# Spectral sequence product: upper rows taken from the lower rows' two sums and one product with the difference of mirrored rows

## Chip, core and metric

The kernel runs on one core of one Trainium2 chip. TensorE (PE) multiplies, ScalarE (ACT), VectorE (DVE) and GpSimd (POOL) work on elements, SyncE (SP) issues all DMAs of the main path from one queue. The metric is the device time of one execution in microseconds (us); the profile's span is the time from the first to the last instruction of one profiled execution.

## Reference

Two independent layers read their own inputs; their outputs stand side by side in a 2048 x 896 result.

```python
S, D, H = 2048, 448, 16
# A: real part of a two-dimensional Fourier transform, by given matrices
a = A_x @ A_dft_hid_re.T
b = A_x @ A_dft_hid_im.T
yA = A_dft_seq_re @ a - A_dft_seq_im @ b
# B: full attention with 16 heads of 28
q, k, v = heads(B_x @ B_wqkv)
yB = concat(softmax(q @ k.T * 28 ** -0.5) @ v) @ B_wo
out = concatenate([yA, yB], axis=-1)
```

The matrices are inputs: `A_dft_seq_re[t, s] = cos(-2 pi t s / 2048)`, `A_dft_seq_im` the sine, in fp32.

## The kernel before

All fp32 data that goes through PE's fast format (`fp32r`) is split into a rounded part `hi` and a rest `lo = x - hi`; a product of two such operands is made of three: hi x hi, hi x lo, lo x hi. The exact fp32 format is used for the sums of attention alone.

Nothing orders the work at run time. While the program is built, a small planner (`Schedule`, L180) keeps a list of tasks for each engine, with a key, a cost and buffers, and emits the instructions in the order in which its own clock lets them run. Each engine then works through its list in that order and waits on semaphores. The costs (`M512`, `M448`, `ACT_S`, ...) and due times (`T_ATT`, `T_END`, `T_FILL`, `T_OUT`, L436) steer only that order.

- **Attention.** For each head, 16 tiles of keys x 4 chunks of 512 queries: a score product (L865), its exponential on ACT (L869), and the sums with v, exact fp32, four 32-row column groups side by side (`quad`, L842, products at L848). The sums are gathered in runs of `run_size` tiles, 8 at first and 10 from 230 us of the plan (`RUN_AT`, L40). `first_tiles` finds each query's offset with transposes and maxima on DVE. `out_of` (L889) takes a head's sums, stores their reciprocals to HBM (L897, L899), reads them spread (L903), multiplies on POOL (L910) and stores the head (L912).
- **Fill.** Everything else on PE fills the gaps between score products: the projections (L581), the values, layer A's transform along the hidden dimension (`hidden`, L682: 16 row tiles of 11 products), and along the sequence (`sequence`, L704). It uses PSUM banks of its own (`fill_s`, `NFILL` = 2).
- **The sequence product.** Part 0 multiplies `wre` by `a`, part 1 `wim` by `-b`. Each part has 16 output tiles of 128 rows; each tile has four steps `q`; each step loads one piece of the matrix (128 x 4 x 128, 256 KB) into `wraw`, splits it (`Piece`, L517: `hi` on ACT L524, `lo` on POOL L530) and issues 12 products of 448 columns (L718). Part 0 stores its tile to HBM (`y_d`, L733); part 1 loads it (L735), adds (L736) and stores the output (L738).
- **Output of attention.** After the last head, for four chunks of 512 rows: load (L967, L972), split (ACT L985, then POOL or DVE), 11 products for each of 16 tiles (L1003), eviction, store (L1011).
- **Check.** A flag (`flag`, L1015) from the sums' and values' ranges decides at the end whether the general path `any_scores` runs instead.

## Time and profile before

| | |
|---|---|
| median of 3 runs | 1010.52 us (1010.41 to 1010.74) |
| the profiled execution | 1010.87 us, its span 1009.2 us |
| granted TensorE clock | 1.000 |
| HBM traffic | 89.92 MB read, 33.69 MB written |
| score exponentials (L869) | 944 in 510.2 us busy |
| sequence products (L718) | 1024 with `whi`, 512 with `wlo` |

The page's busy shares are of the span. A matmul group's mean is the length of one in the pipeline; how far apart they are issued is read from the chain that ended last, printed in order of time.

### The profile page before, as it was taken

Reading aid. Unit: us, or ns where it says so; the run is one execution under the profiler, and the core shown is the slowest. Engines: PE = TensorE matmul, PEld = TensorE weight load, DVE = VectorE, ACT = ScalarE, POOL = GpSimd, SP = SyncE. Lnnn points to the kernel's source line nnn. Section 1 sums busy time; section 2 is a strip of 40 time slices with the busy share of each in tenths; the row PEclk is TensorE's granted clock in tenths of the full one; section 3 lists DMA queues with packets and bytes.
Section 4 is the critical chain, followed back from the end, with each engine's and each line's share of the span. In section 5 each row is a group of like instructions: output and inputs, shape, how many; then the busy total and the mean of one; then the engine's idle time right before and its main releaser. Section 6 shows DMA issues by size and latency. Waiting matters only on the chain.

```text
span 1009.2 us, 16013 instructions
## 1 busy us (share of the span) xinstructions
PE 1002.2 (99%) x5638; PEld 735.8 (73%) x5638; DVE 318.2 (32%) x607; ACT 711.8 (71%) x1410; POOL 364.8 (36%) x339
## 2 busy tenths in 40 slices
PE   9999999999999999999999999999999999999997
PEld 7896667777766876687668666766786677667897
DVE  6362425251505042402314151614041242300111
ACT  7128778798767876796669778877786687667242
POOL 6110234353324333442325443524333253443530
PEclk9999999999999999999999999999999999999999
DMA  8764455324233333333233424242443343243463
GB/s 297 267 202 126 155 180 166 97 77 114 71 100 98 119 89 107 96 114 95 87 104 117 132 67 121 88 118 81 140 104 107 104 141 105 75 125 122 137 198 108
DMA packets 109909, 124.84 MB, mean 124 GB/s; under 512 B 48640, under 2 KB 61440, under 8 KB 109824
## 3 DMA queue, kind: packets, MB, share of 16 engines
q1 hardware_dynamic: 109824, 123.78, 40.7%
q8 instruction: 45, 0.74, 0.3%
q14 instruction: 40, 0.33, 0.1%
HBM read 89.92 MB, written 33.69 MB: 122 GB/s over the span
## 4 chain that ended last, share of the span: by engine, by line
PE 97%; DMA 1%; SPq 0%; DVE 0%; issue 0%; ACT 0%
PE bank L718 31%; PE bank L865 23%; PE bank L848 22%; PE bank L581 16%; PE bank L1003 4%; PE bank L806 1%; DMA kept<-wqkv 1%; DMA kept<-xb 1%; SPq L488 0%; DVE big L427 0%; SPq L559 0%; DVE kept L598 0%; ACT big L490 0%; DVE kept L736 0%
## 5 line engine op out<-in xcount | busy, mean ns | idle before, releaser
L869 ACT ACTIVATE kept<-bank 128x512 f32<-128x512 f32 x944 | 510.2, 678 | 88.8 <-PE bank L865 85.7
L530 POOL TENSOR_TENSOR wlo<-wraw,whi 128x512 fp32r<-128x512 f32 (+1 forms) x164 | 203.1, 1238 | 463.7 <-ACT whi L524 382.0
L865 PE MATMUL bank<-q,k 98*128 98x512 f32 x960 | 328.3, 398 | 0.0
L718 PE MATMUL bank<-big,whi 128*128 128x448 f32 x1024 | 310.8, 367 | 0.0
L848 PE MATMUL bank<-kept,v 128*32 128x512 f32 x2016 | 224.4, 593 | 0.0
L718 PEld LDWEIGHTS bank<-big,whi 128*128 128x128 f32 x1024 | 193.3, 189 | 29.2 <-issue 3.4
L865 PEld LDWEIGHTS bank<-q,k 98*128 98x128 f32 x960 | 180.3, 188 | 44.9 <-issue 11.7
L718 PE MATMUL bank<-big,wlo 128*128 128x448 f32 x512 | 188.3, 368 | 0.0
L848 PEld LDWEIGHTS bank<-kept,v 128*32 128x32 f32 x2016 | 63.5, 110 | 144.4 <-issue 142.3
L524 ACT ACTIVATE whi<-wraw 128x512 fp32r<-128x512 f32 x164 | 114.4, 698 | 22.2 <-PE bank L718 14.7
L718 PEld LDWEIGHTS bank<-big,wlo 128*128 128x128 f32 x512 | 96.7, 189 | 16.9 <-issue 5.9
L837 POOL TENSOR_TENSOR kept<-kept,mb 128x512 f32<-128x512 f32 x51 | 75.7, 1484 | 61.8 <-DVE mb L832 36.5
L581 PE MATMUL bank<-wd,whi 128*128 128x448 f32 x256 | 79.8, 367 | 0.0
L811 DVE STREAM_TRANSPOSE mb<-bank 128x512 f32<-128x512 f32 x64 | 45.8, 715 | 101.4 <-PE bank L806 87.1
L839 ACT ACTIVATE kept<-kept 128x512 f32<-128x512 f32 x64 | 44.7, 771 | 32.9 <-POOL kept L837 30.0
L832 DVE STREAM_TRANSPOSE mb<-am 128x512 f32<-128x512 f32 x64 | 45.5, 711 | 42.4 <-POOL kept L837 41.1
L810 ACT ACTIVATE kept<-bank 128x512 f32<-128x512 f32 x64 | 42.1, 680 | 20.7 <-PE bank L806 20.2
L581 PE MATMUL bank<-big,whi 128*128 128x512 f32 x154 | 52.8, 394 | 0.6 <-DVE kept L598 0.6
L581 PEld LDWEIGHTS bank<-wd,whi 128*128 128x128 f32 x256 | 48.3, 189 | 6.0 <-issue 0.8
L894 ACT ACTIVATE kept<-bank 128x512 f32<-128x512 f32 x16 | 9.5, 596 | 57.6 <-PE bank L848 57.6
L736 DVE TENSOR_TENSOR kept<-bank,kept 128x448 f32<-128x448 f32 x15 | 9.3, 622 | 124.1 <-PE bank L718 110.0
L732 DVE COPY kept<-bank 128x448 f32<-128x448 f32 x16 | 10.0, 624 | 110.7 <-PE bank L718 86.0
(75 smaller groups left out, 753.8 us busy)
## 6 DMA issues: line engine op xcount, KB each, us to landing
wraw<-wre SPq DMA_DIRECT2D x64, 256.0 KB
wraw<-wim SPq DMA_DIRECT2D x64, 256.0 KB
qkd<-kept SPq DMA_DIRECT2D x40, 256.0 KB
wraw<-xa SPq DMA_DIRECT2D x32, 256.0 KB
k<-qkd SPq DMA_DIRECT2D x64, 112.0 KB
q<-qkd SPq DMA_DIRECT2D x64, 112.0 KB
out<-kept SPq DMA_DIRECT2D x31, 224.0 KB
kept<-xb SPq DMA_DIRECT2D x16, 256.0 KB
```

Source lines behind the costliest of these rows:

```text
L524: a = act(key + (0 if early else 1), lambda: nc.scalar.activation(self.hi.t, raw.t, AF.Copy), ACT_S, soon=SOON, deps=[ld], acq=[self.hi], ...
L530: b = sch.add(e, at, lambda g: eng[g].tensor_tensor(self.lo.t[:, :n], raw.t[:, :n], f32(self.hi.t)[:, :n], op=ALU.subtract), deps=[a], acq ...
L581: nc.tensor.matmul(o.t[:, :cols], w(), x(), start=(i == 0), stop=(i == n - 1))
L718: nc.tensor.matmul(o.t[:, :D], a.t[:, k, :], b[:, q * 4 + k, :], start=(q == 0 and k == 0 and j == 0), stop=(q == 3 and k == 3 and j == 2))
L810: made.append(act(key, lambda o=o, s=s: nc.scalar.activation(s.t, o.t, AF.Copy), deps=[m], use=[o, s.pair], lock=[o]))
L811: t = dve(key, lambda o=o, tm=tm: nc.vector.transpose(tm.t, o.t), 0.73, deps=[m], acq=[tm], use=[o], lock=[o], own=RAW_S)
L832: t = dve(key, lambda mb=mb, c=c: nc.vector.transpose(mb.t, f32(am.t)[:, c * NT:(c + 1) * NT].unsqueeze(2).to_broadcast([P, NT, 32])), 0.7 ...
L837: sh = sch.add({"DVE": 0.8, "POOL": POOL_2}, key, lambda e, s=s, mb=mb: eng[e].tensor_tensor(s.t, s.t, mb.t, op=ALU.add), deps=[t, made[c] ...
L839: shown.append(act(key, lambda s=s: nc.scalar.activation(s.t, s.t, AF.Exp, scale=SCALE), ACT_S, deps=[sh], use=[s.pair]))
L848: nc.tensor.matmul(o.t[c * VW:(c + 1) * VW, :], VT[h].t[:, kt // 4, kt % 4, :], tiles[c].t, start=(kt == 0), stop=(kt == NT - 1))
L865: m = pe(key, lambda e, o=o, q=q, kt=kt: nc.tensor.matmul(o.t, KT[h][kt // 4].t[:KM, kt % 4 * P:(kt % 4 + 1) * P], q.t[:KM, :], start=True ...
L869: es[h, kt].append(act(key - 20, lambda o=o, p=p: nc.scalar.activation(p.t, o.t, AF.Exp, scale=SCALE), deps=[m], use=[o, p.pair]))
```

## The change

The sequence matrices are symmetric by row: row 2048 - t equals row t in the real part and is its negative in the imaginary part. Only 8 tiles of rows, t = 0 to 1023, are now multiplied in full, in steps of 16 products: the 12 of before into one bank, and 4 into a second bank with the fp32r rounding of a *difference* piece, the mirrored row minus the row (part 0) or plus it (part 1), and `hi` of the other operand. That difference is computed from both pieces, so both are loaded. The upper row is the lower row's sum plus the difference's product (part 0), minus the lower row's sum plus that product (part 1).

- `Mirror` makes the difference piece: POOL reads the mirrored piece backwards for 127 of 128 columns; the one that lies in the neighbouring tile is kept in `edge` and taken by DVE. DVE also takes the largest absolute value of each difference piece, and once per part of a matrix piece.
- `y_d` holds both rows of a pair; in part 1 the upper tile is stored to `y_d` and copied from there to the output, rows in reverse, HBM to HBM.
- Row 1024 has no partner. `hidden` accumulates its terms on DVE (`acc`, one multiply-add per row tile, with a column of the matrix, `mid`), and one exact product with ones adds up the partitions.
- The flag also requires that no difference exceeds 2^-20 of the matrix's values; otherwise a new general path, `any_sequence`, computes all rows in exact fp32.
- Besides: the sums' runs are of 8 throughout, 20 instead of 22 `kept` buffers, 4 instead of 3 `wraw`, new due times, the fourth chunk of x is split after the first evictions, two splits of the first chunk move from ACT to DVE, and the last output tile is held to the very end and evicted in halves by ACT and DVE. In `any_scores` some operations move between engines.

```diff
-NKEPT = 22
+NKEPT = 20
-RUN_AT = ((0.0, 8), (230.0, 10))
+RUN_AT = ((0.0, 8),)
+SAME = 2.0 ** -20
+NH = NT // 2
-    wraw = new("wraw", [P, 4, P], F32, 3, True)
+    wraw = new("wraw", [P, 4, P], F32, 4, True)
+    wdif = new("wdif", [P, 4, P], F32R, 2, True)
-    T_ATT, T_END, T_FILL, T_OUT = 56.0, 935.0, 1005.0, 950.0
+    T_ATT, T_END, T_FILL, T_OUT = 56.0, 840.0, 920.0, 855.0
...
+    class Mirror:
+        def __init__(self, w, src, key, part, tt, q):
+            op = ALU.add if part else ALU.subtract
+            raw, dif = wraw.slot(), wdif.slot()
+            ld = dma(key, lambda: nc.sync.dma_start(raw.t, src()), acq=[raw])
+            a = pool(key + 1.5, lambda: nc.gpsimd.tensor_tensor(
+                dif.t[:, :, 1:], raw.t[:, :, :0:-1], w.raw.t[:, :, 1:], op=op), deps=[ld, w.ld], acq=[dif], use=[raw, w.raw])
...
+            far_done.append(dve(key + 6, lambda: nc.vector.tensor_reduce(
+                far[:, part, i:i + 1], f32(dif.t).rearrange("p a b -> p (a b)"), axis=AX.X, op=ALU.max, apply_absolute_value=True),
+                0.65, deps=[a, b], use=[dif]))
...
+            acc_done.append(dve(key - 10, lambda o=o, st=st: nc.vector.scalar_tensor_tensor(
+                acc, o.t[:, :D], mid[:, st:st + 1], acc, op0=ALU.mult, op1=ALU.add), 0.62,
+                deps=[end, got, acc_done[-1]], use=[o]))
...
-        for tt in range(NT):
-            o, pair = fill_s.slot(), kept_s.slot()
+        for tt in range(NH):
+            o, o2, pair = fill_s.slot(), fill_s.slot(), kept_s.slot()
...
+                m = Mirror(w, lambda tt=tt, st=st: src[NT - 1 - tt, :, st, :], key - 12.5, part, tt, q)
+                for i in range(16):
+                    if i < 12:
+                        k, j = divmod(i, 3)
                         a, b = ((w.hi, ab_h), (w.hi, ab_l), (w.lo, ab_h))[j]
...
+                    else:
+                        k = i - 12
+                        a, b = m.dif, ab_h
...
+                b1 = dve(key, lambda o=o, y1=y1: nc.vector.tensor_tensor(y1(), o.t[:, :D], y1(), op=ALU.add), 0.62,
+                         deps=[main, ld], use=[o, pair])
+                b2 = dve(key, lambda o=o, y2=y2: nc.vector.tensor_tensor(y2(), y2(), o.t[:, :D], op=ALU.subtract), 0.62,
+                         deps=[main, ld], use=[o, pair])
+                b2 = dve(key, lambda o2=o2, y2=y2: nc.vector.tensor_tensor(y2(), o2.t[:, :D], y2(), op=ALU.add), 0.62,
+                         deps=[b2, last[0]], use=[o2, pair])
+                dma(key, lambda y1=y1, tt=tt: nc.sync.dma_start(out[tt * P:(tt + 1) * P, 0:D], y1()), deps=[b1], use=[pair])
...
+                far_stored = dma(key, lambda y2=y2, tt=tt: nc.sync.dma_start(y_d[tt][:, 1, :], y2()), deps=[b2], use=[pair])
+                half = D // 2
+                dma(key, lambda tt=tt, m0=m0, top=top: nc.sync.dma_start(
+                    bass.AP(tensor=out.tensor, offset=out.offset + top * 2 * D, ap=[[half, 2], [-2 * D, P - m0], [1, half]]),
+                    y_d[tt][m0:, 1, :].rearrange("p (h c) -> h p c", h=2)), deps=[far_stored])
...
-    for c in range(NC):
+    for c in range(3):
         load_x(c, 0.2 + 3 * c if c > 1 else 0.2 + 0.05 * c)
+    after = first_chunks(w_in, (0, 1))
+    load_x(3, 9.2, after)
```

How the instructions stand, at three places. On PE, after the last sums of the last head, the end of one tile and the next; before (`bank_148` and `bank_149` are two tiles of the fill):

```order
L848 MATMUL bank_151<-kept_127,v_111 32x512 x2
L718 MATMUL bank_148<-big,whi 128x448 x2
L718 MATMUL bank_148<-big,wlo 128x448
L718 MATMUL bank_149<-big,whi 128x448 x2
L718 MATMUL bank_149<-big,wlo 128x448
```

and in the changed kernel (L925 are the sums, L779 the sequence products; `bank_146` is the lower row's, `bank_145` the difference's):

```order
L925 MATMUL bank_150<-kept_134,v_110 32x512 x2
L779 MATMUL bank_146<-big,wlo 128x448
L779 MATMUL bank_145<-big,wdif_98 128x448 x4
L779 MATMUL bank_146<-big,whi 128x448 x2
L779 MATMUL bank_146<-big,wlo 128x448
```

The next tile starts in the bank that the last one has just left, four difference products later. From the last sums to the first output product there stand 105 sequence products before and 118 now.

On SP, the DMAs of the last head's sums (`sm`, `rd`) among the pieces' loads; before:

```order
L897 DMA sm_144<-kept_141 128x1x16
L738 DMA out<-kept_125 128x448
L523 DMA wraw_102<-wim 128x512
L523 DMA wraw_103<-wim 128x512
L899 DMA rd_82<-sm_144 128x16
```

and in the changed kernel (L974, L976 and L980 are the sums' transfers, L532 and L564 the pieces and the mirrored pieces, L808 the lower tile, L811 the upper tile to `y_d`, L813 its reversed copy):

```order
L974 DMA sm_141<-kept_132 128x1x16
L808 DMA out<-kept_135 128x448
L811 DMA yd_88<-kept_135 128x448
L532 DMA wraw_93<-wim 128x512
L564 DMA wraw_95<-wim 128x512
L813 DMA out<-yd_88 2x128x224
L976 DMA rd_82<-sm_141 128x16
L532 DMA wraw_94<-wim 128x512
L564 DMA wraw_96<-wim 128x512
L980 DMA kept_132<-rd_82 32x512 x4
```

A store and a copy that waits for it have come between the head's first two transfers.

The end of SP's list, before:

```order
L1011 DMA out<-kept_140 128x448
L1011 DMA out<-kept_121 128x448
L1011 DMA out<-kept_120 128x448
L735 DMA kept_139<-yd_98 128x448
L738 DMA out<-kept_139 128x448
```

and now (L1098 stores attention's output tiles, the last of them `kept_119`):

```order
L1098 DMA out<-kept_126 128x448
L1098 DMA out<-kept_128 128x448
L811 DMA yd_90<-kept_133 128x448
L1098 DMA out<-kept_119 128x448
L813 DMA out<-yd_90 2x128x224
```

The last transfer was a store from SBUF; it is now the reversed copy of the last upper tile, which waits for that tile's store. On PE the last difference product stands 11 output products before the end.

More of the change, by code (lines that the diff above doesn't have):

```diff
@@ L481, in tile_kernel, with load_x @@
     xb_hi, xb_ready = {}, {}
-    def load_x(c, key):
+    def load_x(c, key, after=()):
         cols = slice(c * CH, (c + 1) * CH)
@@ L723, in sequence @@
                         deps += w.ready
+                    if i == 12:
+                        deps += m.ready
                     if tt == 0:
                         deps += [made[q * 4 + k]]
-                    last[0] = pe(key + i * M448, emit, d=M448, deps=deps, acq=[o] if first else [],
-                                 use=[w.hi, w.lo, *([] if first else [o])])
+                    last[0] = pe(key + i * M448, emit, d=M448, deps=deps, acq=[bank] if ends[0] else [],
+                                 use=[*([w.hi, w.lo] if i < 12 else [m.dif]), *([] if ends[0] else [bank])])
@@ L1007, in tile_kernel @@
                 oo = Half(pair, 0)
-                e = sch.add({"ACT": 0.43, "DVE": 0.53}, key, lambda e, o=o, oo=oo: copy_of(e, oo.t[:, :D], o.t[:, :D]),
-                            deps=[m], use=[o, pair])
+                ways = [({"ACT": 0.3}, 0, D // 2), ({"DVE": 0.3}, D // 2, D)] if final else [({"ACT": 0.43, "DVE": 0.53}, 0, D)]
+                e = [sch.add(way, key, lambda e, o=o, oo=oo, c0=c0, c1=c1: copy_of(e, oo.t[:, c0:c1], o.t[:, c0:c1]),
+                             deps=[m], use=[o, pair]) for way, c0, c1 in ways]
                 r0 = c * CH + i * HF + t * P
-                dma(key, lambda oo=oo, r0=r0: nc.sync.dma_start(out[r0:r0 + P, D:], oo.t[:, :D]), deps=[e], use=[pair])
+                dma(key, lambda oo=oo, r0=r0: nc.sync.dma_start(out[r0:r0 + P, D:], oo.t[:, :D]), deps=e, use=[pair])
     fl, fi = kept_s.slot(), new("fi", [1, 1], mybir.dt.int32)
@@ L1029, in tile_kernel @@
         any_scores(tc, qk_d, v_d, on_d, wo, out, kt_s.tiles, q_s.tiles, v_s.tiles, kept_s.tiles, banks, new)
+        any_sequence(tc, xa, wd, wre, wim, out, kept_s.tiles, wraw.tiles + banks, mb_s.tiles[0])
 def any_scores(tc, qk_d, v_d, on_d, wo, out, ks, qs, vs, kept, banks, new):
```

138 lines of the change are left out of this document (103 added, 35 removed).

## The prediction

> **What bounds the kernel now.** I read the page's busy times first, then the chain that ended last, then that chain in order of time, then single stretches.
>
> ```profile
> PE 1002.2 (99%) x5638; PEld 735.8 (73%) x5638; DVE 318.2 (32%) x607; ACT 711.8 (71%) x1410; POOL 364.8 (36%) x339
> PE 97%; DMA 1%; SPq 0%; DVE 0%; issue 0%; ACT 0%
> PE bank L718 31%; PE bank L865 23%; PE bank L848 22%; PE bank L581 16%; PE bank L1003 4%; PE bank L806 1%; DMA kept<-wqkv 1%; DMA kept<-xb 1%; SPq L488 0%; DVE big L427 0%; SPq L559 0%; DVE kept L598 0%; ACT big L490 0%; DVE kept L736 0%
> ```
>
> The chain is PE from the first loads to the last eviction; no other engine has more than a percent of it. So a product removed from PE is a gain at its issue distance, until something else comes late. The distances come from the chain in order of time (start, length, what):
>
> ```profile
> 250.37 7.00 PE bank L848 x64
> 283.15 8.72 PE bank L848 x80
> 938.04 21.47 PE bank L718 x105
> ```
>
> A spectral product of 448 columns is worth 21.47/105 = 0.2045 us. The 0.37 us that groups give as its mean is its length in the pipeline, not its price.
>
> **Products removed.** Two parts x 16 tiles x 48 = 1536 products become 2 x 8 x 64 = 1024: 512 x 0.2045 = **-104.7 us**. All of it lies on the chain.
>
> **Sums in runs of 8.** Before, 7 runs of 8 tiles (x64) and 20 of 10 (x80): 7 x 7.00 + 20 x 8.72 = 223.4 us. After, 32 x 7.00 = 224.0: **+0.6**.
>
> **The middle row.** One exact-fp32 product with one output row is new on PE. Ten tiles of four such 512-column products side by side take 8.72 us; one set of four, 0.87, scaled to 448 columns 0.76. Lower bound: one 0.2045 product. I take the upper, **+0.8**, since it is the same number format.
>
> **The start.** The fourth x chunk now comes behind the first evictions on VectorE.
>
> ```profile
> 21.17 0.72 PE L581 MATMUL bank<-big,whi 128*128 128x512 f32 x2 [0.56 <-DVE kept L598]
> ```
>
> That wait of 0.56 should go: **-0.6** (bounds 0 and -0.6). The two splits that move from ScalarE to VectorE feed a start that waits for its loads, so I give them nothing.
>
> **Work beside PE.** Per group of instructions: busy time, mean ns of one, idle before them.
>
> ```profile
> L530 POOL TENSOR_TENSOR wlo<-wraw,whi 128x512 fp32r<-128x512 f32 x128 | 165.5, 1293 | 350.0 <-ACT whi L524 289.1 <-DMA kept<-rd 19.5 <-PE bank L865 16.8
> L535 POOL TENSOR_TENSOR whi<-wraw,whi 64x128 fp32r<-64x128 f32 x32 | 15.2, 475 | 2.5
> L524 ACT ACTIVATE whi<-wraw 128x512 fp32r<-128x512 f32 x164 | 114.4, 698 | 22.2 <-PE bank L718 14.7 <-DMA wraw<-xa 3.9 <-POOL q L427 0.9
> L812 DVE TENSOR_REDUCE qm<-mb 128x16 f32<-128x512 f32 x64 | 43.7, 682 | 1.9
> L699 DVE SCALAR_TENSOR_TENSOR big<-bank,big 128x448 fp32r<-128x448 f32 x16 | 9.8, 614 | 24.6 <-ACT big L697 24.4
> ```
>
> ScalarE loses 64 splits, 64 x 0.698 = 45 us: 667 of some 915 us, 73%, hardly denser than before (71%), though attention itself runs closer together. GpSimd trades 64 subtractions for 64 mirrored sums or differences, which read a row of 128 backwards. No row shows such a read. Below, 384/512 of the 1.293 us; above, four separate rows of 128, 4 x 0.475 = 1.9. I take 1.3, the nearest in size. VectorE gains 64 maxima (64 x 0.68 = 44 us), 32 multiply-adds (32 x 0.61 = 20) and some 120 small edge operations (about 20): some 400 of 915, 44%. During attention none of this is on the chain, because a step of 16 products is spread among scores there. What hides it is attention's PE work; once that is over, a step lasts 16 x 0.2045 = 3.27 us, and GpSimd needs 1.29 + 1.3 = 2.6 of it. At 1.9 it would need 3.2 and, with the last head's multiplication of 1.29, would come about 1 us late. Loads double per step (two pieces) but not in total. The column load of 2048 four-byte elements is asked for long before its use; I give it nothing.
>
> **A new wait at each tile's end.** Both rows of a tile pair use the first bank, so two VectorE operations read it before the next tile may write.
>
> ```profile
> 1003.65 0.37 PE L718 MATMUL bank<-big,wlo 128*128 128x448 f32 x1
> 1004.06 0.62 DVE L736 TENSOR_TENSOR kept<-bank,kept 128x448 f32<-128x448 f32 x1 [13.36 <-PE bank L718]
> 1004.71 0.33 SPq L738 DMA_DIRECT2D out<-kept  x1
> ```
>
> VectorE starts 0.41 after the product's issue; two operations of 0.62 free the bank at about 1.7. The four difference products leave PE busy only until 5 x 0.2045 = 1.0. So 0.7 late, at the two tile ends after attention's last sums: **+1.4**. During attention score products fill it; without that cover it would be six more in part two, 4 us. Part one has one reader, 0.62: nothing.
>
> **The reversed copies.** Each upper tile goes to HBM and is then copied HBM to HBM, rows in reverse, as 2 x 128 x 224. How many DMA engines carry a transfer with few outer runs is shown by the last head's sums, whose source is 4 partitions. Timeline row, then two windows (us; busy of PE, PEld, DVE, ACT, POOL; clock, DMA share of 16 engines, GB/s):
>
> ```profile
> 938.81 0.61 SPq L897 DMA_DIRECT2D sm<-kept  x1
> 939.90:940.06 0.16, 0.16 (x2) 0.16 (x1) 0.00 (x0) 0.00 (x0) 0.16 (x1) 1.00 0.00 0
> 940.06:940.30 0.24, 0.24 (x3) 0.21 (x3) 0.00 (x0) 0.00 (x0) 0.24 (x1) 1.00 0.24 29
> q1 hardware_dynamic: 109824, 123.78, 40.7%
> ```
>
> In that window 29 GB/s x 0.24 us is 7 KB of this transfer's 8, and 0.24 of 16 engines were busy: four, its outer count. I carry that over: an outer count of 2 gives two engines. The whole queue moved 123.78 MB in 0.407 x 16 x 1009.2 engine-us, 18.8 GB/s each; the copy's 0.229 MB takes 6.1 us on two engines, 0.8 on sixteen. With the mean packet, 59.8 ns, for each of 128 rows it would be 7.7. The Trainium skill, page "DMA: Bandwidth & Descriptors", section "Why a DMA increments its semaphore by 16 and not by 1", says that the engine count is the largest up to 16 that divides the outermost dimension on both sides. By that rule the copy has two engines; the 0.24 agrees.
>
> What it costs at the end:
>
> ```profile
> 1004.70:1005.50 0.80, 0.00 (x0) 0.00 (x0) 0.00 (x0) 0.00 (x0) 0.00 (x0) 1.00 0.00 0
> 1005.50:1007.50 2.00, 0.00 (x0) 0.00 (x0) 0.00 (x0) 0.00 (x0) 0.00 (x0) 1.00 0.34 123
> 1007.50:1009.20 1.70, 0.00 (x0) 0.00 (x0) 0.00 (x0) 0.00 (x0) 0.00 (x0) 0.82 0.02 5
> ```
>
> A store of a tile: 0.8 until data moves, landed after some 2.6, and 1.7 to the span's end. Let T be the end of PE's last product. By the order, the last difference product stands 11 products earlier, T - 2.25. VectorE is done at T - 1.2, the store has landed at T + 1.45, the copy's data start at T + 2.3, last 6.1 and land 0.4 later; the span ends at T + 10.5. Now it ends at T + 5.2: **+5.3** (on sixteen engines about 0; at 7.7, +6.9).
>
> What it costs after attention's last sums:
>
> ```profile
> 943.60 0.38 SPq L899 DMA_DIRECT2D rd<-sm  x1
> 946.75 2.00 SPq L903 DMA_DIRECT2D kept<-rd  x4
> 951.82 1.64 SPq L912 DMA_DIRECT2D ond<-kept  x4
> 959.02 0.72 ACT L985 ACTIVATE q<-kept 128x256 fp32r<-128x256 f32 x2 [2.65 <-DMA kept<-ond]
> ```
>
> The last head's sums pass through HBM three times, and the output's first split starts 959.02 - 938.04 = 21.0 us after the last sums; PE had 105 products, 21.5 us, to cover it. After the change the order gives it 118, 24.1. But on SP a copy stands just ahead of the store of the reciprocals. That store would be issued at about 5.5 as now (the copy waits for its tile until about 5), and its share on the copy's two engines waits until 5.05 + 0.8 + 6.1 = 12.0 instead of 6.3: 5.7 later, and with it all that follows. 21.0 + 5.7 - 24.1 = **+2.6** on PE. Behind the same copy the next pair of pieces lands at about 14 and is split by 16; PE wants it at about 15, a wait inside the 2.6, not beside it. Earlier copies find attention on PE and pieces that were split a step or more ahead; I give them nothing, though each can hold SP's queue some 2.6 us while its tile lands, and loads of pieces, keys and queries are behind it.
>
> **Sum** against the profiled execution: 1009.2 - 104.7 + 0.6 + 0.8 - 0.6 + 1.4 + 5.3 + 2.6 = 914.6. Outside its span it had 1010.87 - 1009.2 = 1.7: 916.3; it was 0.35 above the median of the runs. Forecast **916 us**.
>
> **Rivals.**
> 1. *The copies spread over all engines*, or are otherwise quick. For it: four outer runs of 64-byte pieces may not stand for 896-byte rows. Against it: the row of 0.24. Both copy terms go: 916 - 7.9 = **908**.
> 2. *Pieces become late.* VectorE's edge operations wait for GpSimd's mirrored sum, SP's loads wait for both, and GpSimd also serves the next head's maxima. For it: loads of pieces already waited for GpSimd before.
>
> ```profile
> SPq L523 <- POOL wlo L530: 171.8, 74, 12.9
> ```
>
> Against it: PE lost nothing by that. If the mirrored read costs more than 1.9, each of seven steps after attention is late by the excess, and each copy in attention can let a piece come late by its 6 us: say 1 us x 7 and two of the five copies in attention, 7 + 12, less 5 that the pieces' lead covers: 916 + 14 = **930**.
> 3. *The check sends it into the general path*: slower than before. It decides at one point: any mirrored difference above 2^-20 of the largest value that its partition holds in the first piece. The path has 16 x 4 x 8 rounds with loads; at 2.6 us for one transfer to land that alone is 512 x 2.6 = 1330 us on top, over **2200**. Against it: the reference rounds exact cosines and sines to fp32, so mirrored entries should agree to their last bit.
>
> **Chances.** Forecast with two-engine copies, 911 to 922: 0.52. First rival, 905 to 911: 0.20. Second, 922 to 945: 0.24. Third: 0.02; the other 0.02 for a result near no change. The bounds of the unknown costs (mirrored read +1, tile ends +4, copies 0 to +4 more) lie inside 906 to 930, which leaves out the third, half of the second's upper part and little below. Faster by over 0.2% (about what a measurement of this kernel can tell from no change): 0.97; within 0.2%: 0.01; slower: 0.02.
>
> **What would show it.** In the profile after: 1024 spectral products at 0.2045 in long stretches; the span's last 8 us without PE, with a DMA share of about 2/16 = 0.12 for some 6 of them; a PE wait just before the first output product, released by ScalarE's split; waits of about 0.7 at the two last tile ends; mirrored operations near 1.3 us on GpSimd. A DMA share near 1 for under a microsecond at the end would refute the copy terms; PE waits for mirrored differences during attention would show the second rival; instructions of the general path, the third.

## The result and the profile after

The changed kernel takes **940.66 us** (940.24 to 945.17 in four runs) beside 1010.46 us before on the same chip: a ratio of 0.932, 95% interval 0.9295 to 0.9344. It is faster, as forecast, but 24.7 us slower than the 916 us of the forecast and outside its range. The profiled execution took 945.17 us, its span 943.5 us, so it is itself 4.5 us above the median; its granted clock was 0.989, that of the others 0.992 to 0.994. What is read from its profile is to that extent more than a typical execution lost.

The page of the changed kernel: busy time of the engines, and the chain that ended last by engine and by line.

```profile
PE 919.3 (97%) x5128; PEld 628.8 (67%) x5128; DVE 452.9 (48%) x849; ACT 671.4 (71%) x1344; POOL 334.6 (35%) x333
PE 90%; DMA 3%; DVE 2%; ACT 1%; POOL 1%; issue 1%; SPq 0%; POOLq 0%; ACTq 0%; DVEq 0%
PE bank L925 23%; PE bank L942 23%; PE bank L779 19%; PE bank L623 17%; PE bank L1089 4%; PE bank L659 2%; PE bank L883 2%; DMA wraw<-wre 1%; POOL kept L914 1%; DMA rd<-sm 1%; ACT kept L946 1%; DMA wraw<-wim 1%; DMA wraw<-wo 0%; PE bank L997 0%; ACT whi L533 0%
```

PE carried 97% of the chain before and carries 90% now; what has come in are loads (`wraw`), POOL's additions for the next head (L914) and ScalarE's exponentials (L946) and splits (L533).

**Where the time went.** For every product on PE I took the distance to the next one's issue, less the distance that its form has where nothing waits (0.2045 us for 448 columns, 0.2345 for 512, 0.1075 for each of the sums' products, and the short products of the first 5 us in proportion to their columns). The sum of these differences is called *PE's waits* here (the expectations call it PE's excess); half clock is in it, and so are the turns between the sums and other products, which are most of what the kernel before has. All are of one profiled execution.

| us | before | after | difference | forecast |
|---|---|---|---|---|
| PE's waits, first 100 us | 3.4 | 3.7 | +0.3 | -0.6 |
| PE's waits, 100 to 845 us | 7.0 | 33.8 | **+26.8** | 0 |
| PE's waits, 845 us to the last product | 0.6 | 7.4 | +6.8 | +4.0 |
| from the last product's issue to the end | 5.6 | 10.3 | +4.7 | +5.3 |
| the rest: products, sums, middle row | | | -104.3 | -103.3 |
| span | 1009.2 | 943.5 | -65.7 | -94.6 |

The row "the rest" follows from the prices put in: 512 products of 448 columns fewer and two records for the middle row more. It can't show by itself that the products cost what was forecast. Their issue distances show it: the median of the 448-column products is 0.204 us before and 0.205 after, and the runs of 64 sums on the chain take 7.00 us each but one. So the products went as forecast, the end nearly too, and most of the error lies in the stretch of attention that the forecast took as free of waits.

**How a wait there comes about.** The chain in order of time (start, length, what), between 366 and 380 us:

```profile
by line: DMA wraw<-wre 49.1%; ACT kept L946 14.0%; PE bank L942 13.0%; ACT whi L533 9.0%; PE bank L779 8.9%; SPq L823 3.9%; issue 2.4%; SPq L532 0.4%; SPq L822 0.3%; ACTq L533 0.2%
368.21 0.84 PE bank L779 x4
...
369.14 0.54 SPq L823
...
369.80 3.51 DMA wraw<-wre
...
373.39 0.63 ACT whi L533
374.02 1.96 ACT kept L946 x4
...
376.07 3.36 DMA wraw<-wre
```

and ScalarE in the timeline of the same stretch (in brackets the idle time before and what ended it), then PE:

```profile
368.64 3.15 ACT L946 ACTIVATE kept<-bank 128x512 f32<-128x512 f32 x6
373.39 0.63 ACT L533 ACTIVATE whi<-wraw 128x512 fp32r<-128x512 f32 x1 [1.60 <-DMA wraw<-wre]
373.93 2.53 ACT L946 ACTIVATE kept<-bank 128x512 f32<-128x512 f32 x5
```

```profile
374.56 0.50 PE L942 MATMUL bank<-q,k 98*128 98x512 f32 x1 [1.01 <-ACT kept L946]
```

SP issues the piece's load at 369.80, behind a load of keys (L822 and L823, `k<-qkd`) that had itself waited 3.3 us for PE. It lands 3.5 us later. ScalarE's list has the piece's split next: it stands idle for 1.60 us while the exponentials of finished scores queue up behind the split. The score products' banks are not given back, and PE waits 1.01 us for an exponential. From 100 to 845 us ScalarE stood idle 9.0 us in all before splits of sequence pieces that had not landed; in the kernel before there is no such wait:

```profile
ACT whi L533 <- DMA wraw<-wim: 5.1, 4, 2.1
ACT whi L533 <- DMA wraw<-wre: 3.9, 6, 1.6
```

Over the whole execution, weight loads of score products waiting for exponentials (engine, line, waited for: us in total, times, longest), before and after:

```profile
PEld bank L865 <- ACT kept L869: 5.1, 27, 0.3
```

```profile
PEld bank L942 <- ACT kept L946: 36.1, 145, 1.6
```

**Half clock.** Stretches of the changed kernel (us; busy PE, PEld, DVE, ACT, POOL; granted clock, DMA share, GB/s), and a run of sums of the chain:

```profile
370.50:373.90 3.40, 3.05 (x15) 2.31 (x13) 0.00 (x0) 1.80 (x4) 1.09 (x1) 1.00 0.52 165
751.35:754.77 3.42, 1.69 (x7) 0.72 (x6) 3.25 (x7) 1.33 (x3) 2.11 (x3) 1.00 0.70 239
754.77:758.18 3.41, 3.41 (x17) 0.79 (x20) 2.35 (x4) 3.29 (x7) 1.77 (x2) 0.50 0.39 117
812.79:816.21 3.42, 1.86 (x10) 1.16 (x7) 0.00 (x0) 2.06 (x4) 3.13 (x4) 1.00 0.59 209
816.21:819.62 3.41, 3.41 (x10) 2.82 (x9) 0.25 (x1) 3.41 (x8) 0.50 (x1) 0.50 0.47 117
877.65:881.06 3.41, 0.61 (x4) 0.22 (x2) 0.69 (x1) 0.00 (x0) 2.80 (x3) 1.00 0.70 210
881.06:887.89 6.83, 5.14 (x14) 4.66 (x15) 2.54 (x5) 1.26 (x2) 3.56 (x3) 0.50 0.77 261
```

```profile
754.83 8.67 PE bank L925 x64
```

Three times PE's waits were followed by a granted clock of 0.5, for 3.4, 3.4 and 6.8 us; a run of sums took 8.67 us there instead of 7.00. In this execution 5.6 of the waits stand in these stretches, 3.3 of them before 845 us, which leaves 30.5 of the 33.8 in attention.

**After attention.** Chain, and PE's wait:

```profile
868.32 7.29 DMA rd<-sm
...
875.69 0.34 SPq L980
...
877.51 3.82 DMA kept<-yd
...
882.08 0.54 DVE kept L804
```

```profile
864.89 0.67 PE L779 MATMUL bank<-big,whi 128*128 128x448 f32 x2 [0.49 <-DVE kept L804]
...
882.75 1.09 PE L779 MATMUL bank<-big,whi 128*128 128x448 f32 x2 [4.50 <-DVE kept L804]
```

The copy was issued at 867.59, the store of the reciprocals behind it at 868.32. From there to the spread load (L980) it was 7.37 us; before, from L899 to L903, 3.15. Behind it on SP stood the load of the first part's tile (`yd`): VectorE could not add, and PE's next product came 4.65 us beyond its issue distance. The row at 864.89 is the wait at a tile's end: 0.49 of idle time, 0.65 beyond the issue distance.

**The end.** The last issue on SP, and the windows:

```profile
934.92 0.68 SPq L813 DMA_DIRECT2D out<-yd  x1
```

```profile
935.50:938.50 3.00, 0.00 (x0) 0.00 (x0) 0.00 (x0) 0.00 (x0) 0.00 (x0) 0.53 0.30 95
938.50:942.00 3.50, 0.00 (x0) 0.00 (x0) 0.00 (x0) 0.00 (x0) 0.00 (x0) 0.50 0.13 45
942.00:943.50 1.50, 0.00 (x0) 0.00 (x0) 0.00 (x0) 0.00 (x0) 0.00 (x0) 0.50 0.00 0
```

From 938.5, when the other stores are done, the copy runs alone with 0.13 of 16 engines: two.

### The profile page after: what moved, and what is told of

The parts are those of the page before. It is cut to its first block, busy times and chain, and to the rows that moved or that the text cites. A ratio compares the mean times of both kernels' runs of the same rounds, so it can differ in the third digit from the quotient of the medians.

```text
span 943.5 us, 15195 instructions
## 1 busy us (share of the span) xinstructions
PE 919.3 (97%) x5128; PEld 628.8 (67%) x5128; DVE 452.9 (48%) x849; ACT 671.4 (71%) x1344; POOL 334.6 (35%) x333
## 4 chain that ended last, share of the span: by engine, by line
PE 90%; DMA 3%; DVE 2%; ACT 1%; POOL 1%; issue 1%; SPq 0%; POOLq 0%; ACTq 0%; DVEq 0%
PE bank L925 23%; PE bank L942 23%; PE bank L779 19%; PE bank L623 17%; PE bank L1089 4%; PE bank L659 2%; PE bank L883 2%; DMA wraw<-wre 1%; POOL kept L914 1%; DMA rd<-sm 1%; ACT kept L946 1%; DMA wraw<-wim 1%; DMA wraw<-wo 0%; PE bank L997 0%; ACT whi L533 0%
## 5 line engine op out<-in xcount | busy, mean ns | idle before, releaser
L946 ACT ACTIVATE kept<-bank 128x512 f32<-128x512 f32 x942 | 489.4, 688 | 69.8 <-PE bank L942 58.1
L539 POOL TENSOR_TENSOR wlo<-wraw,whi 128x512 fp32r<-128x512 f32 (+1 forms) x100 | 120.2, 1202 | 349.3 <-ACT whi L533 230.7
L942 PEld LDWEIGHTS bank<-q,k 98*128 98x128 f32 x960 | 179.6, 188 | 95.3 <-ACT kept L946 36.1
L925 PE MATMUL bank<-kept,v 128*32 128x512 f32 x2012 | 226.5, 597 | 0.0
L779 PE MATMUL bank<-big,whi 128*128 128x448 f32 x512 | 169.2, 375 | 5.6 <-DVE kept L804 5.6
L925 PEld LDWEIGHTS bank<-kept,v 128*32 128x32 f32 x2012 | 62.9, 110 | 144.3 <-issue 140.1
L779 PEld LDWEIGHTS bank<-big,whi 128*128 128x128 f32 x512 | 98.4, 193 | 21.6 <-issue 9.0
L565 POOL TENSOR_TENSOR wdif<-wraw,wraw 128x508 fp32r<-128x508 f32 x64 | 71.0, 1110 | 114.2 <-PE bank L779 94.8
L533 ACT ACTIVATE whi<-wraw 128x512 fp32r<-128x512 f32 x100 | 68.2, 682 | 41.0 <-DMA wraw<-wim 27.6
L779 PE MATMUL bank<-big,wlo 128*128 128x448 f32 x256 | 95.6, 373 | 0.0
L779 PE MATMUL bank<-big,wdif 128*128 128x448 f32 x256 | 72.9, 368 | 0.0
L914 POOL TENSOR_TENSOR kept<-kept,mb 128x512 f32<-128x512 f32 x37 | 54.6, 1474 | 41.3 <-DVE mb L909 20.3
L887 ACT ACTIVATE kept<-bank 128x512 f32<-128x512 f32 x64 | 43.4, 726 | 26.4 <-PE bank L883 25.7
L779 PEld LDWEIGHTS bank<-big,wlo 128*128 128x128 f32 x256 | 49.3, 193 | 7.4 <-issue 1.7
L779 PEld LDWEIGHTS bank<-big,wdif 128*128 128x128 f32 x256 | 48.7, 190 | 5.6
```

Source lines behind the costliest of these rows:

```text
L533: a = act(key + (0 if early else 1), lambda: nc.scalar.activation(self.hi.t, raw.t, AF.Copy), ACT_S, soon=SOON, deps=[ld], acq=[self.hi], ...
L539: b = sch.add(e, at, lambda g: eng[g].tensor_tensor(self.lo.t[:, :n], raw.t[:, :n], f32(self.hi.t)[:, :n], op=ALU.subtract), deps=[a], acq ...
L565: a = pool(key + 1.5, lambda: nc.gpsimd.tensor_tensor(dif.t[:, :, 1:], raw.t[:, :, :0:-1], w.raw.t[:, :, 1:], op=op), deps=[ld, w.ld], acq ...
L779: nc.tensor.matmul(bank.t[:, :D], a.t[:, k, :], b[:, q * 4 + k, :], start=ends[0], stop=ends[1])
L887: made.append(act(key, lambda o=o, s=s: nc.scalar.activation(s.t, o.t, AF.Copy), deps=[m], use=[o, s.pair], lock=[o]))
L914: sh = sch.add({"DVE": 0.8, "POOL": POOL_2}, key, lambda e, s=s, mb=mb: eng[e].tensor_tensor(s.t, s.t, mb.t, op=ALU.add), deps=[t, made[c] ...
```

## The experiments

The theories were: **late loads** (two loads per step instead of one come later than the planner's clock says, and the engines' lists stand behind them); **copies** (the reversed copies hold up SP and two DMA engines); **ScalarE's load** (attention runs denser beside the same exponentials); and **VectorE's added work**. All times are medians; waits and tail (from the last product's issue to the end) as above, of one profiled execution each. As that of the changed kernel is 4.5 us above its median, a fall of the waits against its row is overstated by up to that. The column "less tail" is the median less the tail, and is free of it.

| kernel | us | less tail | ratio to before, 95% | waits 100 to 845 | after 845 | tail |
|---|---|---|---|---|---|---|
| changed kernel | 940.66 | 930.4 | 0.9295 to 0.9344 | 33.8 | 7.4 | 10.3 |
| copies in 16 column pieces | 939.38 | 929.2 | 0.9255 to 0.9334 | 31.1 | 6.1 | 10.2 |
| no copies | 930.51 | 925.6 | 0.9188 to 0.9225 | 30.6 | 1.5 | 4.9 |
| landing estimate -0.75 | 944.18 | 933.3 | 0.9314 to 0.9368 | 37.4 | 4.2 | 10.9 |
| landing estimate +1 | 924.91 | 919.3 | 0.9113 to 0.9189 | 22.4 | 4.7 | 5.6 |
| landing estimate +2 | 927.31 | 921.7 | 0.9147 to 0.9200 | 21.1 | 7.4 | 5.6 |
| +1 for pieces alone | 934.13 | 928.5 | 0.9215 to 0.9269 | 27.2 | 7.5 | 5.6 |
| +1 for all but pieces | 933.99 | 928.2 | 0.9214 to 0.9267 | 28.6 | 5.7 | 5.8 |
| before, landing +1 | 1010.62 | 1005.3 | 0.9989 to 1.0012 | 7.3 | 0.5 | 5.3 |
| one load per step | 929.73 | 918.8 | 0.9171 to 0.9224 | 23.9 | 1.8 | 10.9 |
| six raw buffers | 933.43 | 922.5 | 0.9217 to 0.9254 | 27.5 | 2.8 | 10.9 |
| six raw buffers, landing +1 | 929.39 | 923.8 | 0.9184 to 0.9215 | 22.4 | 7.0 | 5.6 |
| sums' runs of 6 | 940.01 | 929.0 | 0.9274 to 0.9328 | 29.7 | 6.7 | 11.0 |
| splits on VectorE | 935.39 | 924.2 | 0.9227 to 0.9280 | 23.6 | 6.8 | 11.2 |
| splits on VectorE, landing +1 | **917.44** | 911.9 | 0.9063 to 0.9094 | 16.5 | 2.9 | 5.5 |
| score copies on VectorE | 945.31 | 934.0 | 0.9327 to 0.9381 | 34.4 | 6.3 | 11.3 |
| score copies on VectorE, landing +1 | 926.56 | 921.0 | 0.9142 to 0.9195 | 22.2 | 5.1 | 5.6 |
| edge operations on GpSimd | 940.36 | 929.8 | 0.9289 to 0.9320 | 28.1 | 8.4 | 10.6 |
| before, runs of 8 and 20 buffers | 1011.99 | 1006.4 | 1.0003 to 1.0026 | 8.2 | 0.9 | 5.6 |

The tail tells where the last copy stands in SP's list: about 10 to 11 where it is the last transfer, under 6 where the planner's order has it earlier or where there is none. So some 5 us of any gain that comes with a short tail are that, and the columns of waits and "less tail" are the cleaner answer to the question of attention.

**The copies.** First all eight copies with an outer dimension of 16 in place of 2.

```diff
-                half = D // 2
+                half = D // 16
-ap=[[half, 2], [-2 * D, P - m0], [1, half]]),
+ap=[[half, 16], [-2 * D, P - m0], [1, half]]),
...
```

> The reversed copy is cut into 16 column pieces (outer count 16 instead of 2); nothing else changes. If the copies on two DMA engines are a large part of the missing 25 us: the copy lands in about 3 us instead of 7.6, the span's end comes some 4.5 us after the last product's eviction earlier, the 4.65 us wait near 878 us goes, and some of the waits after 690 us go: about 928 us or less. If the rest is ScalarE's lack of time in attention: only the end (about 4.5 us) and the wait at 878 us (about 5 us, with the half clock behind it) go: about 930 to 934 us, and PE's excess between 100 and 680 us stays at about 13 us.

939.38 us, outside both expectations: little is gained, and the tail stays. By its packets the data of the last copy, now in runs of 112 bytes, was through 5.7 us after the issue instead of 7.1, but the landing came at 938.3, 7.5 us after the issue at 930.81 (7.6 in the changed kernel). So this run made the copies only a little cheaper; leaving them out removes them:

```diff
-                dma(key, lambda tt=tt, m0=m0, top=top: nc.sync.dma_start(
-                    bass.AP(tensor=out.tensor, offset=out.offset + top * 2 * D, ap=[[half, 2], [-2 * D, P - m0], [1, half]]),
-                    y_d[tt][m0:, 1, :].rearrange("p (h c) -> h p c", h=2)), deps=[far_stored])
+                pass
```

> The eight reversed copies are left out, so the upper rows of the output are not written; everything else stays, with the order that the planner makes without them. The steps of the forecast for the copies were +5.3 at the end and +2.6 after attention. If those are all that copies cost: 930 to 935 us. If copies also hold up loads of pieces during attention: 915 to 928. If the late pieces make up for what the copies leave: 936 to 942.

930.51 us, 10.2 less: by the two profiles 5.3 in the tail and 5.9 after 845 (more than 10.2, as the changed kernel's profiled execution was 4.5 above its median). In attention only 3.2 of 33.8 us went, 2.0 of them half clock, and its chain still stands at the load shown above:

```profile
369.07 3.43 DMA wraw<-wre
...
372.59 0.63 ACT whi L533
```

The copies are a cost of their own after attention and at the end, and not the cause of most waits in attention.

**How long the planner thinks a load takes.** It puts a load's landing at 1.35 us plus its size over 170 behind the issue, 2.86 us for a piece. The loads on the chain above took 3.51 and 3.36, and the one in the kernel without copies 3.43; in attention the changed kernel's chain holds five such loads, of 2.99 to 3.51. The edit acts on every DMA, stores and copies too, and changes only the order of the instructions:

```diff
-                        landed.append(max(at + 1.35 + size / 170 + extra + (3.0 if T_IN - 6 < now < 42 else 0.0), flow + 1.1))
+                        landed.append(max(at + 2.35 + size / 170 + extra + (3.0 if T_IN - 6 < now < 42 else 0.0), flow + 1.1))
```

> The planner takes every DMA to land 1 us later than before; only the order changes. If late loads of pieces that stand in ScalarE's queue ahead of exponentials cost the time: ScalarE's idle time before the piece splits (41 us) falls by half or more, and the time by 5 to 10 us: 931 to 936 us. If ScalarE has no time to spare in attention: within 3 us of 941.

924.91 us. In the stretch shown above, the chain of this kernel has no load and no wait left:

```profile
by line: PE bank L779 51.3%; PE bank L942 43.6%; PE bank L925 3.9%; PE bank L883 3.4%
```

The same place with 3.35, and with 0.6:

> Only the order changes: the planner adds 2 us, not 1, to the landing of every load. Late loads theory: the plan still meets fewer late pieces than the changed kernel's, so 920 to 930 us, with less than 28 us of PE time above its issue distances (40 in the changed kernel) and no half clock during attention. Rival, a lucky order in the run with 1 us: the result is as likely near 940 as near 925; above 935 would speak for it.

> The planner's landing estimate of every load 0.75 us shorter (0.6 in place of 1.35): only the order changes. Late loads theory: the plan meets more late pieces, so slower than the changed kernel, 943 to 960 us, and PE's excess over 40 us. Rival, the order of the changed kernel was merely an unlucky one and the orders with longer estimates lucky ones: 922 to 941.

927.31 and 944.18 us. With 0.6, 1.35, 2.35 and 3.35 the waits in attention are 37.4, 33.8, 22.4 and 21.1: they fall with the estimate and level off, which four unrelated orders need not do. ScalarE's idle time before splits of pieces that had not landed goes the same way, from 14.0 over 9.0 and 5.3 to 0.7 us. But with 3.35, where next to none of it is left, 21.1 us of waits remain: this idle time is one part of the waits, not all. The step from 1.35 to 0.6 is small, its times touch those of the changed kernel. The kernel before, with +1:

> The kernel before with 1 us added to the planner's landing of every load: only the order changes. Late loads theory: one piece per step and a raw buffer per piece in three steps leave room, PE already loses only 6 us there, so 1009 to 1013 us. Rival, the estimate was simply too low for this chip and any kernel would gain: below 1006.

1010.62 us, no difference: with one load per step and three buffers, a longer estimate had nothing to gain. Then whose loads. Pieces alone (`extra=1.0` at the two loads of `Piece` and `Mirror`), and all others alone, stores and copies among them (2.35, with `extra=-1.0` there):

> 1 us added to the landing estimate of the spectral pieces' loads alone; keys, queries, values, sums and copies keep theirs. If the late loads that matter are the pieces': 920 to 931 us. If they are the others': 934 to 943.

> The other half: 1 us added to the landing estimate of every load but the spectral pieces'. If the late loads that matter are the pieces': 934 to 943 us. If they are the others' (keys, queries, values, the sums' passes through HBM): 920 to 931.

934.13 and 933.99 us: each lies at the edge of the range in which its half is not what matters. Without the tail the halves gain 1.9 and 2.2 us, the full edit 11.1. (The waits of the profiles fall by 6.6, 5.2 and 11.4, but 3.3 of each fall is the half clock of the changed kernel's execution.) So neither the pieces' loads alone nor the others alone account for the gain; it takes both, and the runs don't divide it between them. Both kinds stand in SP's one list.

**Loads and buffers.** The mirrored piece's load left out:

```diff
-SAME = 2.0 ** -20
+SAME = 2.0 ** 20
...
-            raw, dif = wraw.slot(), wdif.slot()
+            raw, dif = w.raw, wdif.slot()
...
-            ld = dma(key, lambda: nc.sync.dma_start(raw.t, src()), acq=[raw])
+            ld = w.ld
```

> The load of the mirrored piece is left out: the difference or sum is made from the piece itself read backwards, so the upper rows are not the reference's, and the bound of the check is raised so that the same path runs. Loads per step and raw buffers per step are then as before (one, out of four); GpSimd, VectorE, ScalarE and the copies keep all their work. Late loads theory with the loads' number as the cause: PE's excess falls below 28 us and the time to 918 to 930 us. If the chain of GpSimd and VectorE behind each piece is the cause, or the engines' load: 935 to 943.

929.73 us with the tail still at 10.9, so 11.6 less without the tail: waits in attention fall by 9.9 (6.6 without the half clock) and behind it by 5.6, and ScalarE's idle time before late pieces from 9.0 to 0.8 us. All engines' work and all copies were still there, so the second load per step, with its buffer and its place in SP's list, is what made pieces late at ScalarE. The run also halves the number of pieces' loads in all (64 instead of the 128 of both kernels), which it can't tell from the load per step. And 23.9 us of waits remain, 7.0 before. More buffers:

```diff
-    wraw = new("wraw", [P, 4, P], F32, 4, True)
+    wraw = new("wraw", [P, 4, P], F32, 6, True)
-NKEPT = 20
+NKEPT = 19
...
```

> Six raw buffers for pieces instead of four, one pair of the kept buffers less; the planner's landing estimate and the two loads per step stay, so a load may be asked for up to three steps ahead instead of two. Late loads theory with too few buffers as the place: 918 to 930 us, PE's excess under 28 us. If the buffers are not what makes pieces late, but the time that the plan allows a load: 934 to 943.

> Six raw buffers and 1 us more in the planner's landing of every load. If both act on the same late pieces: 920 to 926 us, little below the 925 of the landing edit alone. If they are two separate causes: 912 to 919. A slower result than 930 would say that an order's luck is worth more than either.

933.43 us, between the two expectations, with waits of 27.5: six buffers are three for each load of a step, as many as the kernel before had, and most of the waits remain. With the longer estimate 929.39 us, outside every expectation and 4.5 us slower than the estimate alone (the times of the two kernels' runs don't overlap). Buffers help less than the estimate does and don't add to it; that an order's chance alone is worth some 4 us is not excluded.

**ScalarE: its load or its list.** Shorter runs of sums (`RUN_AT = ((0.0, 6),)`) need banks and exponentials in smaller bunches:

> The sums run in 43 runs of up to 6 tiles instead of 32 of 8. PE pays about 11 x 0.4 us more in turns, 4 us. If ScalarE's time is the bound of attention: it idles about 4.8 us in each run of 7 us because only six banks of scores are ahead of it; in runs of 5.25 us it idles about 3, so some 20 us of idle time go and attention gets shorter: 925 to 935 us. If late loads or copies cost the time: about 945 us.

940.01 us, no difference, and outside both expectations. The piece's first split on VectorE:

```diff
-            a = act(key + (0 if early else 1), lambda: nc.scalar.activation(self.hi.t, raw.t, AF.Copy), ACT_S, soon=SOON,
+            a = dve(key + (0 if early else 1), lambda: nc.vector.tensor_copy(self.hi.t, raw.t), 0.43, soon=SOON,
```

> The first split of each piece is made by VectorE instead of ScalarE, so a piece that lands late no longer stands in ScalarE's queue ahead of the exponentials; loads, buffers and copies stay. Late loads theory, by way of ScalarE's queue: the waits of score products for ScalarE shrink and the time is 918 to 930 us. If late pieces stop PE directly, through the spectral products: 933 to 943. If VectorE's small operations are what comes late: slower than 943.

935.39 us, in the range given for late pieces that stop PE directly, though attention's waits fell from 33.8 to 23.6, as expected for the way by ScalarE's list. Without the tail the gain is 6.2 us. This could be relief of ScalarE just as well (623.5 us busy instead of 671.4), so as a control other work of ScalarE that never waits for a load goes to VectorE:

```diff
-            made.append(act(key, lambda o=o, s=s: nc.scalar.activation(s.t, o.t, AF.Copy), deps=[m], use=[o, s.pair], lock=[o]))
+            made.append(dve(key, lambda o=o, s=s: nc.vector.tensor_copy(s.t, o.t), 0.53, deps=[m], use=[o, s.pair], lock=[o]))
```

> The 64 copies of a head's first score tiles go from ScalarE to VectorE: ScalarE loses 43 us of work that waits for products and never for loads; the pieces' splits stay on ScalarE. If the splits on VectorE helped because they no longer hold up the exponentials behind a late load: 938 to 944 us here. If they helped because ScalarE had less to do: 932 to 937. If VectorE's longer chain ahead of each head costs more: over 945.

945.31 us, waits 34.4: nothing gained. It is just in the third range, in which VectorE's longer chain ahead of each head costs more, so by its time alone it does not tell the other two apart. The two side by side with the longer estimate:

> The landing edit of 1 us and the first split of each piece on VectorE. If ScalarE's queue is one more way on which late pieces reach PE: 918 to 924 us. If the landing edit already keeps late pieces out of ScalarE's queue: 923 to 928. If VectorE's queue then becomes the way: above 928.

> The same together with 1 us more in the planner's landing of every load. If ScalarE's load matters once the pieces are less late: 917 to 921 us, as with the splits on VectorE. If the splits' place in ScalarE's queue matters: 923 to 929, as with the landing edit alone.

917.44 and 926.56 us, beside 924.91 for the estimate alone. Score products waiting for exponentials, for the score copies on VectorE, the splits on VectorE, and the splits with the longer estimate:

```profile
PEld bank L942 <- ACT kept L946: 36.7, 121, 5.2
```

```profile
PEld bank L942 <- ACT kept L946: 16.7, 73, 1.0
```

```profile
PEld bank L942 <- ACT kept L946: 13.0, 59, 1.1
```

A ScalarE that is lighter by 29.6 us (641.8 busy instead of 671.4) leaves the sum of these waits as it was, 5.2 us of it in a single wait; taking the splits, which wait for loads, out of its list halves them. With the longer estimate too, the score copies gain nothing and the splits 7.5 us. This speaks for the list and against the load. It is not a clean proof: the splits relieve ScalarE by 47.9 us and the copies by 29.6, and the copies lengthen VectorE's chain. The kernel with both edits is the fastest of all here, 23 us faster than the changed kernel, 4.8 of them by the shorter tail.

**VectorE's small operations.** The edge operations of 128 x 4 elements (lines 568 and 574) are on the chain with 1.1 to 1.2 us each; the changed kernel's groups by line (min/median/max ns):

```profile
L568 DVE TENSOR_TENSOR wdif<-edge,wraw x56: 103/168/1272, 301.9 to 891.9; 128x4 fp32r<-128x4 f32 x56
L574 DVE COPY edge<-wraw x56: 115/515/1244, 244.8 to 876.1; 128x4 f32<-128x4 f32 x56
```

With both on GpSimd (`pool(...)` and `nc.gpsimd` at these two places):

> The two edge operations of each mirrored piece (128 x 4 elements) go from VectorE to GpSimd; everything else is the changed kernel. On VectorE 52 of the 112 lasted 0.35 to 1.3 us and each of these ended within 0.06 us of the end of the GpSimd operation beside it; the others took 0.1 to 0.25. If this holding up of VectorE is a main way on which PE waits arise: PE's excess between 100 and 845 us falls from 34 to under 27 and the time to 925 to 934 us. If it only lengthens work that lies beside PE: 936 to 943. If GpSimd becomes what comes late: over 945.

940.36 us, no difference, though they take 0.2 us there and VectorE's busy time falls from 452.9 to 396.0 us. The waits read 28.1 in attention (30.5 in the changed kernel without half clock), but 8.4 behind it. This holding up of VectorE lies beside PE.

**Runs of 8 in the kernel before** (`RUN_AT = ((0.0, 8),)`, `NKEPT = 20`):

> The kernel before with two parts of the change alone: runs of 8 throughout and 20 instead of 22 kept buffers. If the buffers or the shorter runs cost time by themselves: 1015 us or more. By the sum of the prediction, 0.6 us of turns: about 1011 us. If shorter runs help ScalarE only where it has no time left, which it has here: also about 1011 us.

1011.99 us, ratio 1.0014 (1.0003 to 1.0026): +1.5 us, between 0.3 and 2.6. The sums' runs and buffers are not the cause.

## Why the prediction was right or wrong

- **Products removed, sums, middle row: right.** 512 sequence products went, at an issue distance that stayed at 0.2045; the middle row's product took 0.84 us to the next issue for 0.8 forecast; runs of 8 with 20 buffers cost the kernel before 1.5 us (0.3 to 2.6) for 0.6.
- **The start: the named wait went, and the clock hid it.** PE no longer waits for L598. But its first products, after and before:

```profile
5.56 1.62 PE L659 MATMUL bank<-big,whi 128*128 128x512 f32 x3
5.28 0.98 PE L616 MATMUL bank<-big,whi 128*128 128x512 f32 x3
```

  In this execution the first four are issued 0.37 to 0.56 us apart, about twice the later 0.23, until 7.25 us, where the trace's record of the full clock begins; in the kernel before that record begins at 5.08. This costs 0.7 us more than before without any wait of PE, and 0.3 more stand ahead of the first of them. Together they outweigh the wait that went: +0.3, not -0.6.
- **The mirrored read: right in kind, smaller in size.** 1.11 us, not 1.3:

```profile
L565 POOL TENSOR_TENSOR wdif<-wraw,wraw 128x508 fp32r<-128x508 f32 x64 | 71.0, 1110 | 114.2 <-PE bank L779 94.8
```

- **The wait at a tile's end: right.** 0.65 us, for 0.7 forecast. The second one is part of the 4.65.
- **The copy at the end: right.** Two engines by the share of 0.13; +4.7 for +5.3. By the rule of the Trainium skill, page "DMA: Bandwidth & Descriptors", section "Why a DMA increments its semaphore by 16 and not by 1", which the forecast cites, two was the number too.
- **The copy after attention: right in mechanism, wrong in place.** The spread load came 4.2 us later (7.37 less 3.15) for 5.7 forecast, but what PE waited for was not the output's split: it was the tile of the first part, whose load stands behind that chain on SP. 4.65 us instead of 2.6, and the clock fell to half behind it. Both copy terms together: 7.9 forecast, 10.2 by the kernel without copies.
- **"During attention none of this is on the chain, because a step of 16 products is spread among scores there": this is the step that failed.** It put the waits in attention at nothing: it counted engines' busy time against PE's, and the loads as "double per step (two pieces) but not in total". The total is indeed not the point; SP's and ScalarE's lists are worked in order, and a late load stops a list. The runs showed 26.8 us of waits there, of the 28.9 by which the profiled span missed the forecast's 914.6. ScalarE stood idle 9.0 us before pieces that had not landed, which it did not in the kernel before, and score products' weight loads waited 36.1 us for exponentials instead of 5.1. Of the 26.8, 3.3 are half clock of this execution; 14.0 went when the plan allowed every DMA 1 us more and the split left ScalarE's list (30.5 to 16.5); 9.5 remained. So for about half of the error, late loads and the order of the lists are shown by runs; for the 9.5 the cause stays open.
- **The second rival named this outcome and not its mechanism or size.** It had pieces late by the copies and at seven steps after attention, 14 us in all. The measured time lies in its range of 922 to 945, but by another way: in the run without copies ScalarE still stands idle 8.4 us before late pieces, and the lateness was spread over all of attention. What spoke against it, that PE lost nothing by late loads before, held for the kernel before only (no difference with +1 there).
- **The first and third rivals** are refuted: two engines, and no instruction of the general path.

What stays open: the kernel with both edits still has 16.5 us of waits in attention, 7.0 before. Its score products' weight loads still wait 13.0 us for exponentials, 5.1 before; why was not tried. Nor was it measured why a 256 KB load takes 3.4 us at those moments and not the plan's 2.9.

## What to carry to other kernels

When a change adds loads or other in-order entries per step without adding time to any engine, price the entries as waits in every list that they stand in: what lies behind a load-bound entry on ScalarE or SP waits with it, whatever the engine's busy share. An order that was planned with fixed latencies has a slack that the old kernel's profile doesn't show; here 1 us on the latency of every DMA, and moving the load-bound step off the engine that PE depends on, were worth 23 us, 5 of them at the end. The reversal was written with an outer dimension of 2 and ran on two engines: don't let such a transfer be the last one.

## What the runs showed of the hardware

- **The clock can fall after waits that fill half of a stretch of 3.4 us.** PE was busy for 1.69 of 3.42 us, 1.86 of 3.42 and 0.61 of 3.41 before the three stretches at 0.5; with 3.05 of 3.40 it stayed at 1.00. The busy share alone does not decide it: in the run with +1 for all but pieces, a stretch with 1.70 of 3.42, a whole number of 3.413 us ahead of that run's later fall, was followed by the full clock:

```profile
696.95:700.37 3.42, 1.70 (x8) 1.14 (x6) 2.91 (x6) 0.67 (x2) 1.08 (x1) 1.00 0.69 187
700.37:703.78 3.41, 2.50 (x18) 1.41 (x22) 0.00 (x0) 3.41 (x8) 1.90 (x2) 1.00 0.63 201
```

  The Trainium skill, page "TensorE: Matmul & The Clock Gate", section "What's actually happening", puts the half rate after an idle window of about 3.4 us; the lengths (3.4, 3.4, 6.8) agree with such windows, but two windows that were half busy were enough here.
- **VectorE waits for GpSimd.** Of the 112 edge operations of 128 x 4, 54 lasted 0.30 to 1.27 us; all 54 began during an operation of GpSimd and ended within 0.06 us of its end. The other 58 took 0.10 to 0.17, and only two of them began during one. The forecast had some 20 us for all of them; they took 60 (26.0 and 34.2 us busy). The Trainium skill, page "GPSIMD Engine Reference", section "Specifications", has GpSimd's SBUF interfaces shared with VectorE, contended by instructions in a 2-port mode or with two SBUF inputs; the operations of line 568 have two such inputs and agree, the copy of line 574 has one, and whether it runs in a 2-port mode no run here shows.
- **A copy in 16 pieces was through sooner, but the last one landed no sooner.** By the packets of the eight copies, the data in 16 pieces of 112-byte runs was through 4.2 to 6.0 us after the issue, in 2 pieces of 896-byte runs 6.9 to 8.3. The last copy landed 7.5 us after its issue in 16 pieces, 1.8 us behind its last packet, and 7.6 us in 2 pieces, 0.5 behind it. What held up the landing no run shows.
